# An attention and feed-forward kernel: the place of group 1's attention, of the splits of weights, and of second products behind first products

## The chip, the cores and the metric

The kernel runs on one core of one Trainium2 chip. The metric is the device time of one execution in microseconds (us). Before the change it is 775.43 us, the median of 3 runs (774.27 to 777.92).

## The reference

Attention with 4 sink keys and a causal window of 128 keys, then a feed-forward stage without gate. All arrays are float32 but the two weight matrices, which arrive as float64 (512 KB for a block of 128 x 512).

```python
# q, k, v: (4 batches, 8 heads, 768, 64)
scores = q @ k.T / 8;  keep = (key < n_sink) | (0 <= query - key < window)
a = softmax(where(keep, scores, -1e9));  attn = a @ v
x = attn, heads side by side             # (3072, 512)
h = x @ w_in                             # (3072, 2048)
g = h * erf(softplus(h))
out = g @ w_out                          # (3072, 512)
```

## The kernel before

**Groups and slots.** The 3072 tokens are 12 groups of 256 (three per batch). A group has 4 attention steps, one for each pair of heads (step s belongs to group s // 4), and 16 slots of the feed-forward stage, one for each block of 128 hidden columns. Slot m of the loop has the first product of block f = m % 16 of group m // 16 (`hidden`); every second slot the activation of two blocks (`act`); and the second product of slot m - 4 (`project`, LAG = 4). Ten slots of attention alone (LEAD) stand ahead, so the planner's slot number is a = m + 10.

**Two forms of the products.** Group 0's first products, and the second products of groups 0 and 1, are float32 matmuls (L606, L649). All others are made of three rounded (fp32r) matmuls each, of high and low parts (L610; L652 to L654). They need each weight block split in two: a cast to the high part on ScalarE and a subtraction on VectorE (`wsplit`, L527 and L528). Before that, the 32 blocks are converted from float64 bits to float32 by three VectorE instructions each (`wconv`, L511, L516, L519). Blocks 0 to 15 are w_in's, 16 to 31 w_out's. Splits 0 to 15 have the slots m = 11 to 26, splits 16 to 31 the slots m = 24 to 46 (`split`).

**A step of attention.** `prep` transposes q and k on TensorE (L281), ScalarE copies them to kq. `score` multiplies on TensorE (L329); VectorE merges halves (L341) and adds the mask with a row maximum (L346); ScalarE takes the exponent (L350). `norm` divides (L357 to L369; steps 4 to 7 have the four products on ScalarE, L363). `ptrans` transposes the probabilities (L381, L382); ScalarE copies them (L385, L390), GpSimd cuts triangles out of them (L395). `av` multiplies with v (L422). `xfin` makes x: for group 0 one copy (L435), for others a high part on ScalarE (L440) and a low part on VectorE (L441). Group g's first products read x of all its four steps, in 4 chunks of contraction, one chunk per step.

**What sets the order.** `pos(s)` is a step's slot, and `plan` holds the parts of a step with their slots. Steps 0 to 3 (NE = 4) have slots 0 to 3, with `av` three slots after `score` and `xfin` four. From step 4 on, the slots are 4 apart (5, 9, 13, 17, 21, ...), and `av` of step s stands directly before the scores of step s + 2 (AL = 2; `core`, L289). Each part gets a priority key by `at`: 256 times its slot, plus an offset by kind (O: scores -300, preparation -100, activation -400, first product 0, splits +300, second product +900). The build's planner lays out each engine's queue from these keys and from what it takes to be ready; each engine then works through its queue in that order. `follow(prev, ins)` ties an instruction behind another of the same queue, without a semaphore.

**Buffers.** First products have two PSUM tiles (tag h), each for two slots; a tile comes free when VectorE's first multiplication of the activation (L631, i = 0) has read it. Second products have two tiles (tag o), one group's; transposes, preparation and `av` share two (tag t). Weights, their splits and the inputs of groups 0 and 1 (k_early, q_early, v_early) share 33 buffers (wpool). SyncE issues all loads in one queue, among them copies of v to vz, which `av` reads: `next_dup` (L248, L250) for group 1, in slot 8.

Of the kernel before, what the change touches and what calls it, by code (L numbers as in the profile page):

```python
# [9 lines left out]
F32 = mybir.dt.float32  # L10
# [3 lines left out]
AF = mybir.ActivationFunctionType  # L14
ALU = mybir.AluOpType
# [14 lines left out]
CC = (-0.3597576685435788, 7.2931830957863735, 0.5777779046187317)  # L30
CK = 0.018644221205607978
CS = CK ** (1 / 6)
# [7 lines left out]
NE, AL = 4, 2  # L40
# [12 lines left out]
def kernel(  # L53
# [11 lines left out]
    nc = tc.nc  # L65
# [3 lines left out]
    NPAIR = H // 2  # L69
# [8 lines left out]
    scale = 1.0 / math.sqrt(D)  # L78
# [8 lines left out]
    b_a = [CS * a for a in CA]  # L87
# [38 lines left out]
    wf, wt = {}, {}  # L126
# [4 lines left out]
    def fast_path():  # L131
        with ExitStack() as st:
# [19 lines left out]
                out=kw[:, :256], in0=rf[:, :256], scalar=0.0, in1=kw[:, :256], op0=ALU.is_ge, op1=ALU.mult  # L152
# [27 lines left out]
            xp, early = {}, {}  # L180
# [108 lines left out]
            def core(s):  # L289

                prev = None
                late = s - AL >= NE
                if late:
                    prev = av(s - AL)
                if s < NSTEP:
                    score(s, prev)
# [150 lines left out]

            def pos(s):

                return s if s < NE else 4 * s - 11  # L450

            plan = {}
            for s in range(NSTEP + AL):
                if s < NSTEP:
                    for what, fn, a in (
                        ("prep", prep, pos(s) - (3 if s < NE or s >= 2 * NPAIR else 1)), ("norm", norm, pos(s) + 1), ("ptrans", ptrans, pos(s) + 2),
                        ("load", load, pos(s) - 4),
                    ):
                        if what == "load":
                            if s < 2 * NPAIR:  # L460
                                continue
                            plan.setdefault(a, []).append(("load", load_v, s))
                        plan.setdefault(max(a, 0 if what == "prep" else -1), []).append((what, fn, s))
                    if s >= 2 * NPAIR:
                        plan.setdefault(pos(s) - 2, []).append(("dup", dup, s))
                    if s // NPAIR % GPB < GPB - 1:
                        plan.setdefault(pos(s) + (2 if s < NE else 1), []).append(("kcopy", kcopy, s))
                plan.setdefault(pos(s), []).append(("core", core, s))
                if s < NE:
                    plan.setdefault(pos(s) + 3, []).append(("av", av, s))  # L470
                    plan.setdefault(pos(s) + 4, []).append(("xfin", xfin, s))
                elif s - AL >= NE:
                    plan.setdefault(pos(s) + 1, []).append(("xfin", xfin, s - AL))
            STAGES = ("av", "xfin", "norm", "ptrans", "kcopy", "prep", "core", "dup", "load")

# [44 lines left out]
                    out=ti, in0=w[:, :, 0], scalar=29, in1=ti, op0=ALU.logical_shift_right, op1=ALU.bitwise_or  # L520
                )

            def wsplit(n):

                t = wf[n]
                d = wt[n] = wpool.tile([P, 2, DM], F32R, tag="wo", name=f"wt_{n}")
                nc.scalar.copy(d[:, 0, :], t)  # L527
                nc.vector.tensor_tensor(d[:, 1, :], t, d[:, 0, :].bitcast(F32), op=ALU.subtract)  # L528

            def wblock(n):  # L530
                if n < 16:
# [4 lines left out]
            mlp = make_mlp(work, ps_h, ps_o)  # L536
            wn, wl = 0, W0
            gs = {}
# [13 lines left out]
            for m in range(-LEAD, NG * NF + LAG + 2):  # L552
                a = m + LEAD
                live = 0 <= m < NG * NF
                if live:
                    g, f = divmod(m, NF)
                    if f % 2 == 0:
                        hp = mlp.hid_tile(m)
                    if f > 0:
                        with at(a, "hid"):  # L560
                            mlp.hidden(hp, xp[g], f)
                attn(a)
                w = m - LAG
                if 0 <= w < NG * NF:
                    g2, f2 = divmod(w, NF)
                    with at(a, "proj"):
                        mlp.project(gs[w // 2], g2, f2)
                    if f2 == NF - 1:
                        for i in range(2):
                            r0 = (g2 * 2 + i) * P  # L570
                            with at(a, "res"):
                                nc.sync.dma_start(out[r0 : r0 + P, :], mlp.result(g2, i))
                if live:
                    if f == 0:
                        with at(a, "hid"):
                            mlp.hidden(hp, xp[g], f)
                    if f % 2 == 1:
                        with at(a, "act"):
                            gs[m // 2] = mlp.act(hp, m, g < 2)

                while wn < 32 and a >= 1 and (wn < (0, 1, 3, 5)[a - 1] if a < 5 else wn < 2 * a - 4 or need(order[wn]) <= m + W1):
                    with at(a, "wc"):
                        wconv(order[wn], wn)
                    wn += 1
                    with at(a, "wl"):
                        for n in order[wl : wn + WQ]:
                            wload(n)
                            wl += 1
                for n in split.get(m, ()):
                    with at(a, "ws"):  # L590
                        wsplit(n)

    class make_mlp:
        def __init__(self, work, ps_h, ps_o):
            self.work, self.ps_h, self.ps_o = work, ps_h, ps_o
            self.acc = {}

        def hid_tile(self, m):
            return self.ps_h.tile([P, 2, GT], F32, tag="h", name=f"h_{m}")
# [1 line left out]
        def hidden(self, hp, xt, f):  # L601
            j, fs = f // 4, slice(f % 4 * P, f % 4 * P + P)
            o = hp[:, f % 2, :]
            if len(xt) == 1:
                for c in range(NC):
                    nc.tensor.matmul(o, wf[NC * j + c][:, fs], xt[0][:, c, :], start=(c == 0), stop=(c == NC - 1))  # L606
                return
            ops = [(c, *e) for c in range(NC) for e in ((0, 0), (0, 1), (1, 0))]
            for m, (c, p, e) in enumerate(ops):
                nc.tensor.matmul(  # L610
                    o, wt[NC * j + c][:, p, fs], xt[e][:, c, :], start=(m == 0), stop=(m == len(ops) - 1)
                )

        def act(self, hp, m, whole=False):
            work = self.work
            h = hp.rearrange("p a t -> p (a t)")
            r = work.tile([P, 512], F32, tag="r", bufs=1, name=f"r_{m}")
            if whole:
                acc = work.tile([P, 2, 512], F32, tag="g", bufs=2, name=f"gf_{m}")[:, 0, :]
            else:  # L620
                acc = None
            nc.scalar.activation(r, h, AF.Tanh, bias=b_t, scale=0.5)  # L622
            nc.scalar.activation(r, r, AF.Square, bias=b_v, scale=-0.5)  # L623
            nc.scalar.activation(r, r, AF.Square, bias=b_r)  # L624
            for i in range(3):
                u = work.tile([P, 512], F32, tag="u", bufs=UB, name=f"u{i}_{m}")
                nc.scalar.activation(u, r, AF.Square, bias=b_a[i], scale=CS)  # L627
                x = h if i == 0 else acc
                if acc is None:
                    acc = u  # L630
                nc.vector.scalar_tensor_tensor(out=acc, in0=u, scalar=CC[i] * CS**2, in1=x, op0=ALU.add, op1=ALU.mult)  # L631
            if whole:
                return (acc,)
            gt = work.tile([P, 2, 512], F32R, tag="g", bufs=2, name=f"g_{m}")
            gh, gl = gt[:, 0, :], gt[:, 1, :]
            nc.vector.tensor_copy(gh, acc)  # L636
            nc.gpsimd.tensor_tensor(gl, acc, gh.bitcast(F32), op=ALU.subtract)  # L637
            return gh, gl

        def project(self, gt, g, f):  # L640
            if f == 0:
                for i in range(2):
                    self.acc[g, i] = self.ps_o.tile([P, DM], F32, tag="o", name=f"o_{g}_{i}")
            for i in range(2):
                o = self.acc[g, i]
                n0 = (f % 2) * GT + i * P
                ws = slice(n0, n0 + P)
                if len(gt) == 1:
                    nc.tensor.matmul(o, gt[0][:, ws], wf[16 + f], start=(f == 0), stop=(f == NF - 1))  # L649
                    continue  # L650
                gh, gl = gt
                nc.tensor.matmul(o, gh[:, ws], wt[16 + f][:, 0, :], start=(f == 0), stop=False)  # L652
                nc.tensor.matmul(o, gh[:, ws], wt[16 + f][:, 1, :], start=False, stop=False)  # L653
                nc.tensor.matmul(o, gl[:, ws], wt[16 + f][:, 0, :], start=False, stop=(f == NF - 1))  # L654

# [151 lines left out]
```

## Time and profile before

| | |
|---|---|
| median of 3 runs | 775.43 us |
| the profiled execution, whole | 773.4 us |
| its span, first to last instruction | 771.6 us |
| TensorE busy | 728.0 us (94%) |
| VectorE busy | 496.0 us (64%) |
| ScalarE busy | 549.2 us (71%) |
| GpSimd busy | 202.4 us (26%) |
| mean granted TensorE clock | 0.978 |

Busy times are of one profiled execution. TensorE's matmuls are pipelined, so that the length of one says less than the distance from one start to the next. "Idle before" is an engine's empty time ahead of an instruction, with what ended it. A share over the whole span mixes the opening, in which weights come in and are converted, with ten groups that look alike.

### The profile page before, as it was taken

How to read it: one execution, taken by the hardware profiler on the slowest of the kernel's cores; microseconds unless marked ns; L12 is line 12 of the kernel's file. 1: busy time of each engine (PE TensorE's matmuls, PEld its weight loads, DVE VectorE, ACT ScalarE, POOL GpSimd, SP SyncE). 2: the span in 40 equal slices, each digit the busy share in tenths (PEclk: the TensorE clock that was granted, in tenths of full speed). 3: DMA queues.
4: the chain of work that ended last, by engine and by line, in shares of the span. 5: the costliest groups of instructions: out<-in, count | busy, mean ns of one | idle time of the engine just before them, and what ended most of it. 6: DMA issues, size and time to landing. Idle time of an engine off the chain costs nothing. (4 is left out here: it accounts for less than half of the span.)

```text
span 771.6 us, 16346 instructions
## 1 busy us (share of the span) xinstructions
PE 728.0 (94%) x5808; PEld 603.5 (78%) x5808; DVE 496.0 (64%) x1375; ACT 549.2 (71%) x1293; POOL 202.4 (26%) x281
## 2 busy tenths in 40 slices
PE   6689946999999999999999999999999999999997
PEld 3456624776788888888888888888888888888895
DVE  7999983566477476476476476476476476576352
ACT  4476855887597588588598587587597597597572
POOL 1220102201233332232242242242242242242221
PEclk9899969999999999999999999999999999999999
DMA  9999002211122122122222222212212212210000
GB/s 196 257 330 364 15 0 45 66 39 34 41 69 52 49 57 56 48 51 51 55 51 61 53 51 59 51 47 55 55 48 61 55 49 57 52 34 1 29 1 32
DMA packets 115112, 53.59 MB, mean 69 GB/s; under 512 B 93840, under 2 KB 107664, under 8 KB 115024
## 3 DMA queue, kind: packets, MB, share of 16 engines
q1 hardware_dynamic: 114192, 52.33, 25.8%
q8 instruction: 49, 0.80, 0.4%
q14 instruction: 39, 0.32, 0.1%
q10 hardware_dynamic: 832, 0.13, 0.1%
HBM read 38.54 MB, written 6.29 MB: 58 GB/s over the span
## 5 line engine op out<-in xcount | busy, mean ns | idle before, releaser
L610 PE MATMUL h<-xh,wt 128*128 128x256 f32 x1408 | 273.0, 284 | 10.3 <-DVE gf L631 7.3
L610 PEld LDWEIGHTS h<-xh,wt 128*128 128x128 f32 x1408 | 223.3, 188 | 19.0 <-DVE gf L631 7.2
L610 PE MATMUL h<-xl,wt 128*128 128x256 f32 x704 | 198.3, 283 | 0.0
L627 ACT ACTIVATE u<-r 128x512 f32<-128x512 f32 x288 | 161.5, 622 | 9.9 <-DVE gf L631 2.2
L637 POOL TENSOR_TENSOR g<-u,g 128x512 fp32r<-128x512 f32 x80 | 104.1, 1302 | 241.7 <-DVE g L636 216.7
L610 PEld LDWEIGHTS h<-xl,wt 128*128 128x128 f32 x704 | 132.3, 188 | 4.8 <-issue 1.0
L395 POOL TENSOR_SCALAR_AFFINE_SELECT pz<-pa 64x256 f32<-64x256 f32 x96 | 52.1, 543 | 313.2 <-ACT pa L385 310.0
L652 PE MATMUL o<-wt,g 128*128 128x512 f32 x320 | 129.5, 405 | 0.1
L631 DVE SCALAR_TENSOR_TENSOR u<-u,u 128x512 f32<-128x512 f32 x160 | 119.0, 744 | 15.9 <-ACT u L627 1.0
L653 PE MATMUL o<-wt,g 128*128 128x512 f32 x320 | 127.9, 400 | 0.0
L654 PE MATMUL o<-wt,g 128*128 128x512 f32 x320 | 124.5, 399 | 0.3 <-POOL g L637 0.2
L631 DVE SCALAR_TENSOR_TENSOR u<-u,h 128x512 f32<-128x512 f32 x80 | 54.9, 686 | 81.0 <-ACT u L627 75.5
L350 ACT ACTIVATE pst<-pst,neg 128x144 f32<-128x144 f32 x192 | 77.6, 406 | 15.1 <-DVE neg L346 13.2
L622 ACT ACTIVATE r<-h 128x512 f32<-128x512 f32 x96 | 57.0, 594 | 41.5 <-PE h L610 34.1
L654 PEld LDWEIGHTS o<-wt,g 128*128 128x128 f32 x320 | 59.0, 188 | 12.7 <-POOL g L637 0.6
L653 PEld LDWEIGHTS o<-wt,g 128*128 128x128 f32 x320 | 60.2, 188 | 11.0
L652 PEld LDWEIGHTS o<-wt,g 128*128 128x128 f32 x320 | 60.2, 188 | 10.7 <-issue 0.3
L649 PE MATMUL o<-wf,gf 128*128 128x512 f32 x128 | 60.2, 613 | 3.2 <-DVE gf L631 3.2
L624 ACT ACTIVATE r<-r 128x512 f32<-128x512 f32 x96 | 60.7, 633 | 2.7
L623 ACT ACTIVATE r<-r 128x512 f32<-128x512 f32 x96 | 61.0, 635 | 2.0
L636 DVE CAST g<-u 128x512 fp32r<-128x512 f32 x80 | 36.4, 455 | 36.1 <-PE o L654 32.8
L441 DVE TENSOR_TENSOR xl<-av,xh 128x256 fp32r<-128x256 f32 x44 | 18.5, 420 | 55.5 <-ACT xh L440 54.9
(85 smaller groups left out, 968.3 us busy)
## 6 DMA issues: line engine op xcount, KB each, us to landing
ws<-in_moe_w_in_dram SPq DMA_DIRECT2D x16, 512.0 KB, 6.7
ws<-in_moe_w_out_dram SPq DMA_DIRECT2D x16, 512.0 KB, 9.0
out_dram<-ot SPq DMA_DIRECT2D x24, 256.0 KB, 2.2
v<-in_v_dram SPq DMA_DIRECT2D x56, 96.0 KB, 2.4
q<-in_q_dram SPq DMA_DIRECT2D x80, 64.0 KB, 2.1
k<-in_k_dram SPq DMA_DIRECT2D x80, 64.0 KB, 2.1
vz<-v SPq DMA_DIRECT2D x80, 64.0 KB, 2.1
kq<-kq SPq DMA_DIRECT2D x28, 64.0 KB, 1.9
```

Of the source, the lines that this page charges most:

```text
L350: nc.scalar.activation(y, y, AF.Exp, bias=d["neg"][:, i, h : h + 1], scale=-1.0, accum_out=d["sum"][:, i, h : h + 1])
L610: nc.tensor.matmul(o, wt[NC * j + c][:, p, fs], xt[e][:, c, :], start=(m == 0), stop=(m == len(ops) - 1))
L622: nc.scalar.activation(r, h, AF.Tanh, bias=b_t, scale=0.5)
L623: nc.scalar.activation(r, r, AF.Square, bias=b_v, scale=-0.5)
L624: nc.scalar.activation(r, r, AF.Square, bias=b_r)
L627: nc.scalar.activation(u, r, AF.Square, bias=b_a[i], scale=CS)
L631: nc.vector.scalar_tensor_tensor(out=acc, in0=u, scalar=CC[i] * CS**2, in1=x, op0=ALU.add, op1=ALU.mult)
L637: nc.gpsimd.tensor_tensor(gl, acc, gh.bitcast(F32), op=ALU.subtract)
L649: nc.tensor.matmul(o, gt[0][:, ws], wf[16 + f], start=(f == 0), stop=(f == NF - 1))
L652: nc.tensor.matmul(o, gh[:, ws], wt[16 + f][:, 0, :], start=(f == 0), stop=False)
L653: nc.tensor.matmul(o, gh[:, ws], wt[16 + f][:, 1, :], start=False, stop=False)
L654: nc.tensor.matmul(o, gl[:, ws], wt[16 + f][:, 0, :], start=False, stop=(f == NF - 1))
```

## The change

There are three parts. First, group 1's four steps (4 to 7) get the slots 6, 9, 12, 15 instead of 5, 9, 13, 17; their preparation moves to the slots 4, 4, 5, 6 (before: 4, 8, 12, 16); their `av` stands three slots after their scores, and `xfin` four (slots 10, 13, 16, 19), as for group 0, where before `av` waited for the scores of two steps later (`xfin` in the slots 14, 18, 22, 26). Second, the two instructions of a split of slot m are tied behind the last square (ScalarE) and the last multiplication (VectorE) of an activation some two to three slots earlier. Third, for slots m of group 2 and later, except the first of each group, the first matmul of each half of the second product of slot m - 4 is tied behind the last matmul of slot m's first product.

```diff
-                late = s - AL >= NE
+                late = s - AL >= 2 * NPAIR
...
-                return s if s < NE else 4 * s - 11
+                return s if s < NE else 3 * s - 6 if s < 2 * NPAIR else 4 * s - 11
...
-                        ("prep", prep, pos(s) - (3 if s < NE or s >= 2 * NPAIR else 1)), ("norm", norm, pos(s) + 1), ("ptrans", ptrans, pos(s) + 2),
+                        ("prep", prep, max(4, s - 1) if NE <= s < 2 * NPAIR else pos(s) - 3), ("norm", norm, pos(s) + 1), ("ptrans", ptrans, pos(s) + 2),
...
-                if s < NE:
+                if s < 2 * NPAIR:
                     plan.setdefault(pos(s) + 3, []).append(("av", av, s))
                     plan.setdefault(pos(s) + 4, []).append(("xfin", xfin, s))
-                elif s - AL >= NE:
+                elif s - AL >= 2 * NPAIR:
...
-            def wsplit(n):
+            def wsplit(n, m):
...
-                nc.scalar.copy(d[:, 0, :], t)
-                nc.vector.tensor_tensor(d[:, 1, :], t, d[:, 0, :].bitcast(F32), op=ALU.subtract)
+                x, y = mlp.mark[(m - 1) // 2 - 1]
+                follow(x, nc.scalar.copy(d[:, 0, :], t))
+                follow(y, nc.vector.tensor_tensor(d[:, 1, :], t, d[:, 0, :].bitcast(F32), op=ALU.subtract))
...
-                            mlp.hidden(hp, xp[g], f)
+                            ahead = mlp.hidden(hp, xp[g], f)
...
-                        mlp.project(gs[w // 2], g2, f2)
+                        mlp.project(gs[w // 2], g2, f2, lambda ins: follow(ahead if live and f and g >= 2 else None, ins))
...
+            if isinstance(m, int):
+                self.mark[m // 2] = sq, pr
...
-        def project(self, gt, g, f):
+        def project(self, gt, g, f, behind=lambda ins: ins):
...
-                nc.tensor.matmul(o, gh[:, ws], wt[16 + f][:, 0, :], start=(f == 0), stop=False)
+                behind(nc.tensor.matmul(o, gh[:, ws], wt[16 + f][:, 0, :], start=(f == 0), stop=False))
```

## Rows read from the trace of the kernel before

**Rows 1.** The page's busy tenths of TensorE and VectorE and the granted clock, in 40 slices of 19.3 us.

```profile
PE   6689946999999999999999999999999999999997
...
DVE  7999983566477476476476476476476476576352
...
PEclk9899969999999999999999999999999999999999
```

**Rows 2.** Busy time by stage: stretch, its length, busy us (instructions) of TensorE, its weight loads, VectorE, ScalarE and GpSimd, granted clock, share of the DMA engines, GB/s.

```profile
0.00:41.40 41.40, 27.00 (x228) 17.20 (x228) 35.15 (x131) 18.58 (x62) 10.33 (x25) 0.92 0.94 238
41.40:97.70 56.30, 53.47 (x242) 35.85 (x243) 55.88 (x121) 42.91 (x93) 8.03 (x8) 0.97 0.66 223
97.70:146.90 49.20, 31.79 (x260) 22.00 (x260) 29.01 (x89) 27.74 (x77) 6.98 (x15) 0.79 0.10 24
146.90:204.40 57.50, 57.50 (x413) 39.99 (x408) 34.63 (x101) 43.79 (x106) 7.55 (x14) 1.00 0.20 48
204.40:765.97 561.57, 558.21 (x4672) 488.50 (x4670) 341.38 (x937) 415.58 (x956) 169.46 (x220) 1.00 0.20 48
```

**Rows 3.** TensorE's instructions in order of time, 97 to 141 us: start, us, engine, line, operation, tiles, shape, count, and idle time before with what ended it.

```profile
97.70 0.35 PE L610 MATMUL h<-xh,wt 128*128 128x256 f32 x1 [0.92 <-DVE gf L631]
...
104.68 0.58 PE L610 MATMUL h<-xh,wt 128*128 128x256 f32 x1 [6.38 <-DVE gf L631]
...
108.88 9.41 PE L649 MATMUL o<-wf,gf 128*128 128x512 f32 x16 [3.20 <-DVE gf L631]
...
121.17 0.99 PE L329 MATMUL ps<-kq 64*64 64x208 f32 x16
...
126.59 0.33 PE L381 MATMUL tp<-ident,pst 128*128 128x128 f32 x1 [3.15 <-ACT pst L363]
...
140.83 0.48 PE L610 MATMUL h<-xh,wt 128*128 128x256 f32 x2
```

**Rows 4.** VectorE's groups of instructions in the stretch 97.7 to 147.9 us: count, busy us, mean ns, idle before.

```profile
L528 DVE TENSOR_TENSOR wt<-wf,wt 128x512 fp32r<-128x512 f32 x18 | 12.2, 717 | 9.4 <-ACT wt L527 9.3
L346 DVE CUSTOM_DVE_ANT_0 pst<-ps,mask 128x144 f32<-128x144 f32 x16 | 4.0, 304 | 0.1
L341 DVE COPY_PREDICATED ps<-tri,ps 64x256 f32<-64x256 int8 x8 | 3.4, 431 | 0.8 <-PE ps L329 0.6
...
L441 DVE TENSOR_TENSOR xl<-av,xh 128x256 fp32r<-128x256 f32 x3 | 1.2, 416 | 4.2 <-ACT xh L440 4.2
```

**Rows 5.** ScalarE in order of time, 88 to 105 us.

```profile
88.01 5.84 ACT L527 CAST wt<-wf 128x512 fp32r<-128x512 f32 x11
...
104.06 0.63 ACT L627 ACTIVATE u<-r 128x512 f32<-128x512 f32 x1
```

**Rows 6.** The casts of splits (L527) on ScalarE alone, by stage: stretch, length, busy us (count), clock, DMA.

```profile
41.40:97.70 56.30, 7.59 (x14) 0.97 0.66 223
97.70:111.00 13.30, 4.20 (x7) 0.58 0.00 0
...
146.90:204.40 57.50, 4.32 (x7) 1.00 0.20 48
```

**Rows 7.** Distances between starts on TensorE at full clock: 14 matmuls of a float32 second product (66.58 to 72.59); `av`, scores and preparation of one step (431.02 to 433.30); 24 matmuls of first products (435.94 to 438.77); the transposes of probabilities (439.71, 440.14).

```profile
66.58 6.17 PE L649 MATMUL o<-wf,gf 128*128 128x512 f32 x14
72.59 3.62 PE L606 MATMUL h<-xf,wf 128*128 128x256 f32 x16
...
431.02 0.55 PE L422 MATMUL av<-pa,v 128*64 128x128 f32 x8
...
433.30 0.48 PE L652 MATMUL o<-wt,g 128*128 128x512 f32 x1
...
435.94 0.40 PE L610 MATMUL h<-xh,wt 128*128 128x256 f32 x2
...
438.77 0.39 PE L654 MATMUL o<-wt,g 128*128 128x512 f32 x1
...
439.71 0.60 PE L381 MATMUL tp<-ident,pst 128*128 128x128 f32 x4
440.14 0.27 PE L382 MATMUL ts<-ident,snk 128*128 128x128 f32 x1
```

**Rows 8.** A boundary between two groups in the steady part, all engines in order of time.

```profile
429.53 0.39 PE L652 MATMUL o<-wt,g 128*128 128x512 f32 x1
...
432.49 0.42 DVE L441 TENSOR_TENSOR xl<-av,xh 128x256 fp32r<-128x256 f32 x1 [4.89 <-ACT xh L440]
...
440.81 0.39 PE L610 MATMUL h<-xh,wt 128*128 128x256 f32 x1 [0.40 <-DVE u L631]
```

**Rows 9.** The table of TensorE's waits over the whole span: the row of the first products behind a PSUM tile in use (waiting instruction, releaser: us in total, times, longest).

```profile
PE h L610 <- DVE u L631: 3.0, 8, 0.4
```

**Rows 10.** The instructions on vz: the issues of `next_dup` (count, ns of an issue, first and last start), and the time from issue to landing of all copies to vz (shortest, median, longest).

```profile
L250 SPq DMA_DIRECT2D vz<-v_early x2: 461/698/935, 51.6 to 53.8; - x2
...
DMA to landing us min/median/max: 1.5/2.1/10.6
```

**Rows 11.** GpSimd and VectorE in order of time, 81 to 85 us.

```profile
81.69 1.76 POOL L395 TENSOR_SCALAR_AFFINE_SELECT pz<-pa 64x256 f32<-64x256 f32 x2 [21.92 <-ACT pa L385]
...
83.19 1.61 DVE L516 SCALAR_TENSOR_TENSOR wf<-ws,wf 128x512 int32<-128x512 int32 x2
```

**Rows 12.** All 32 conversions of one kind (ns: shortest, median, longest; first and last start).

```profile
L516 DVE SCALAR_TENSOR_TENSOR wf<-ws,wf x32: 668/692/893, 20.9 to 94.5; 128x512 int32<-128x512 int32 x32
```

More of the change, by code (lines that the diff above doesn't have):

```diff
@@ L590, in fast_path @@
                     with at(a, "ws"):
-                        wsplit(n)
+                        wsplit(n, m)
     class make_mlp:
@@ L595, in __init__ @@
             self.work, self.ps_h, self.ps_o = work, ps_h, ps_o
-            self.acc = {}
+            self.acc, self.mark = {}, {}
         def hid_tile(self, m):
@@ L609, in hidden @@
             for m, (c, p, e) in enumerate(ops):
-                nc.tensor.matmul(
+                last = nc.tensor.matmul(
                     o, wt[NC * j + c][:, p, fs], xt[e][:, c, :], start=(m == 0), stop=(m == len(ops) - 1)
                 )
+            return last
         def act(self, hp, m, whole=False):
@@ L626, in act @@
                 u = work.tile([P, 512], F32, tag="u", bufs=UB, name=f"u{i}_{m}")
-                nc.scalar.activation(u, r, AF.Square, bias=b_a[i], scale=CS)
+                sq = nc.scalar.activation(u, r, AF.Square, bias=b_a[i], scale=CS)
                 x = h if i == 0 else acc
@@ L630, in act @@
                     acc = u
-                nc.vector.scalar_tensor_tensor(out=acc, in0=u, scalar=CC[i] * CS**2, in1=x, op0=ALU.add, op1=ALU.mult)
+                pr = nc.vector.scalar_tensor_tensor(out=acc, in0=u, scalar=CC[i] * CS**2, in1=x, op0=ALU.add, op1=ALU.mult)
+            if isinstance(m, int):
+                self.mark[m // 2] = sq, pr
             if whole:
```

## The prediction

> **What bounds the kernel now.** I read four views in this order. The page's busy tenths [rows 1] show TensorE at nine tenths or more from the eighth slice to the last but one. Ahead of that, behind an opening of "66899", stands one hole, the digits "46" of the sixth and seventh slices, about 96 to 135 us; the granted clock falls there too. So the steady part is bounded by TensorE itself, and what can be won lies before some 147 us. The sums by stage [rows 2] put numbers to this. From 146.90 to 765.97 us TensorE is idle for 3.4 of 619 us. In the stretch 97.70 to 146.90 it is busy for 31.79 of 49.2 us, at a granted clock of 0.79: part of the stretch is at the lower level (1.2 GHz), so that even the busy time is stretched. Just before, from 41.40 to 97.70, VectorE is full (55.88 of 56.3) and TensorE nearly so (53.47).
>
> TensorE in order of time [rows 3] shows what the hole is made of. Group 1's first products begin at 97.70 and stop after a few matmuls; the bulk starts at 140.83. Between lie the scores of step 7 (121.17) and transposes that wait for ScalarE: x of group 1 isn't ready, since its last two attention steps run one after the other with nothing beside them. They are late because VectorE and ScalarE were given something else first. ScalarE casts 11 splits in a row from 88.01 on, and the last square of an activation of group 0 is done only after 104.06 [rows 5]; 21 of the 32 casts are done by 111 us [rows 6], when group 1 needs four of them to begin. VectorE subtracts 18 splits after 97.70, 12.2 us of its time [rows 4]. The idle times of 0.92, 6.38 and 3.20 us at 97.70, 104.68 and 108.88 all end with group 0's activations, which stood in that queue.
>
> **What the hole is worth.** I price its work at full clock by the distances of [rows 7]. 16 float32 second products at (72.59 - 66.58)/14 = 0.43 us make 6.9. 48 matmuls of first products (slots 16 to 19) at (438.77 - 435.94)/24 = 0.118 make 5.7. Four attention steps, each with `av`, scores and preparation of 433.30 - 431.02 = 2.28 and transposes of 0.43 + 0.27 = 0.70, make 11.9. That is 24.5 us of work in 49.2 us [rows 2]: 24.7 us are lost, 17.4 as idle time and the rest to the clock. This is the most that the first two parts of the change can give back there.
>
> **Part 1, group 1's attention.** No instruction is added. Step 5 to 7's preparation no longer stands behind the transposes of the step before, and `av` no longer behind the scores of two steps later; x of group 1 is due in slot 19 instead of 26. The work goes under the stretch from 41.40 on. Its costs, where none can gain unless an end below 0 says so:
> - Three preparations go ahead of group 0's first products. TensorE is idle for 14.4 us of the first 41.40 and ScalarE for 22.8 [rows 2], which hides them. Ends -1.5 (they fill idle time) and +2 (the copies of group 0's x queue behind them on ScalarE). I take 0.
> - VectorE's share of steps 6 and 7 moves ahead of 97.70: per step (4.0 + 3.4)/4 + 1.2/3 = 2.25 us for the three larger kinds [rows 4], 4.5 for both, some 6 with the small kinds. The engine is full there, so conversions and activations behind them come later; TensorE is covered as far as these were ahead of use. Subtractions that leave the stretch give back 0.68 each. Ends -1 and 6.4; I take 3.
> - `av` of step 4 reads vz, whose copies for group 1 are issued at 51.6 to 53.8 us and land up to 10.6 us later [rows 10], at 64.4. The SyncE queue and slot 8 of these copies are unchanged, and the slot of this `av` falls from 13 to 9. TensorE works its queue in order: score, products and transposes behind a waiting `av` wait as well. Ends 0 and 6; I take 1.5. Freed earlier, k_early and q_early give buffers back to the loads of weights, which can only help.
> - GpSimd's cuts of steps 6 and 7 now run beside a full VectorE. At 83.19, under a GpSimd run, two conversions take 1.61 us [rows 11] against 0.692 each in the median and 0.893 at the longest [rows 12]: 0.2 us more for each instruction that is caught. Some five per step make 2 us for two steps. Ends 0 and 2; I take 1.
>
> The Trainium skill's GPSIMD Engine Reference, section Specifications, says that GpSimd shares its SBUF interfaces with VectorE, with contention for VectorE instructions that have two SBUF inputs. By that rule the subtractions and activations beside the cuts would slow down too; the trace agrees as far as the 0.893 against 0.692 goes, and the sum would end 2 us later than without any contention.
>
> **Part 2, the splits.** The ties keep splits 0 to 7 behind activations of group 0 and send the others, of which some 13 were done by 111 us, into group 1's time. This frees ScalarE around 88 to 107 us and lets the last two activations of group 0 go as their products end, so the 16 second products follow at once. Splits 8 to 23 then fall into group 1: 16 casts against 7 in 146.90 to 204.40 [rows 6], 9 x 0.62 = 5.6 us more on ScalarE, 49.4 of 57.5 us [rows 2]. That is 86%, close enough for some waits: ends 0 and 6, I take 1.5. At the start of group 1 both PSUM tiles are filled after four slots and the next waits for the first activation; the 6.9 us of group 0's second products cover that if they are still there. Ends 0 and 3, I take 1.
>
> **Part 3, second products behind first products.** In most slots the keys (offset 900, so 3.5 slots) put a second product behind the first product of four slots ahead anyway, and the tie changes nothing. It bites at a group's end: second products of blocks 13 to 15 now stand before the next group's first products of slots 1 to 3 (one of them at 429.53, before x is whole at 432.49 + 0.42) [rows 8], and will stand behind them. Then the new group's first activation starts earlier, and the wait of 0.40 us at 440.81 for a PSUM tile [rows 8] goes; there are 8 of these, 3.0 us in all [rows 9]. For filling the time before x is whole, three of four chunks of the first products of four slots remain. Ends: a gain of 4 (ten boundaries at 0.40) and a loss of 42 (18 matmuls at (439.71 - 438.77)/4 = 0.235 [rows 7], 4.2 us a boundary, all uncovered, at ten boundaries). I take a gain of 2, near the measured wait, because 432.91 lies before the 433.30 at which TensorE is through with scores and preparation.
>
> **The sum.** 24.7 - (0 + 3 + 1.5 + 1 + 1.5 + 1) + 2 = 24.7 - 8.0 + 2 = 18.7 us. The profiled execution took 773.4 us, so 754.7; the median shown is 775.43, 2.0 above it, so I predict 756.7, rounded to 757. What is late next is VectorE until about 106 us, then TensorE.
>
> **Rivals.**
> - *The hole shrinks only.* VectorE has no slack under 41.40 to 97.70 and the costs of parts 1 and 2 come at their upper ends, two thirds of them: 16 us in place of 8, part 3 nothing. 773.4 - 24.7 + 16 = 764.7, with the 2.0 about 767 (762 to 771). For it: 55.88 of 56.3 busy. Against it: 12.2 us of subtractions leave the queue behind.
> - *The change doesn't do what it says.* The scores of steps 4 to 7 move by only +1, 0, -1 and -2 slots, and the planner's queues may hold them as late as before: 775. For it: step 7, of slot 17, was scored at 121.17, long after the first product of slot 26 (m = 16) had begun at 97.70 [rows 3], so slots alone don't place it. Against it: that was the serial order of transposes, preparation and `av`, which is gone.
> - *Slower: part 3 drains TensorE at every boundary.* Its place is between the last matmul that needs no fourth chunk and the moment x is whole, in each of the ten boundaries; its price up to 4.2 us each. It decides from 18.7/10 = 1.9 us a boundary. At half the price, 21 us, the time is 773.4 - 24.7 + 8.0 + 21 + 2.0 = 780; at the full price 801. For it: one second product is used just there now, at 429.53. Against it: the four slots' three chunks hold 36 matmuls, 4.2 us, of which part is used already.
>
> **How the numbers follow.** My forecast has a chance of 0.58 (748 to 762), the smaller gain 0.24, no effect 0.08, slower 0.10. Less than 0.5% (3.9 us) can't be told from no change: faster 0.82, same 0.08, slower 0.10. The low end takes all 24.7 us, part 3's 4 and no cost: 773.4 - 28.7 + 2.0 = 746.7, hardly to be had, so 748; the high end takes in the smaller gain: 771.
>
> **What would show it.** Right: scores of step 7 before 97 us, a granted clock near 1.00 from 97 to 147 us, no run of 11 casts, fewer than ten casts by 100 us, and the wait at a PSUM tile after each boundary gone. Wrong: first products of group 1 still starting after 115 us; TensorE idle around 58 to 64 us behind vz for more than 3 us; a new wait of first products for xl at each boundary; ScalarE above nine tenths in group 1 with TensorE waiting for it.

## The result, and the profile after

The changed kernel takes 750.03 us (median of 4 runs, 748.57 to 750.50) against 776.67 us before (4 runs, 774.27 to 778.52): a ratio of 0.9655, with a 95% interval of 0.9622 to 0.9689. The profiled execution took 750.17 us, 23.2 less than the 773.4 of before. The predicted 757 was 7 us too high; the range of 748 to 771 holds the time. One execution of part 1 alone, at 893.04 us and a mean granted clock of 0.752, is left out of that kernel's median and ratio below.

The busy tenths of the changed kernel, which answer to [rows 1]:

```profile
PE   6589899999999999999999999999999999999996
...
DVE  7999896565786665666665665666576576475252
...
PEclk9899999999999999999999999999999999999999
```

The hole at the sixth and seventh slices is gone, and so is the drop of the clock. VectorE's line is no longer full up to the sixth slice and then empty: it has been evened out. Busy time by stage, which answers to [rows 2]; the columns are the same:

```profile
0.00:41.40 41.40, 26.48 (x212) 17.19 (x212) 35.38 (x132) 19.22 (x63) 10.84 (x25) 0.92 0.94 243
41.40:97.70 56.30, 50.85 (x316) 34.56 (x317) 53.47 (x134) 39.73 (x102) 21.19 (x17) 0.97 0.70 225
97.70:146.90 49.20, 49.20 (x334) 34.45 (x333) 35.88 (x95) 40.84 (x95) 4.01 (x8) 1.00 0.17 41
146.90:204.40 57.50, 55.83 (x431) 40.61 (x430) 36.56 (x106) 44.02 (x110) 10.75 (x18) 1.00 0.22 52
```

From 97.70 to 146.90 TensorE is busy for all of 49.20 us at a clock of 1.00 (31.79 and 0.79 before). Ahead of it, its idle time has grown from 2.8 to 5.5 us, and GpSimd's busy time has grown from 8.03 to 21.19 us for 17 instructions. TensorE in order of time, which answers to [rows 3]:

```profile
61.29 0.99 PE L329 MATMUL ps<-kq 64*64 64x208 f32 x16
...
84.60 0.34 PE L422 MATMUL av<-pa,v_early 128*64 128x64 f32 x4 [1.92 <-POOL pa L395]
...
107.82 0.68 PE L611 MATMUL h<-xh,wt 128*128 128x256 f32 x1
...
194.86 0.40 PE L656 MATMUL o<-wt,g 128*128 128x512 f32 x1
```

Step 7 is scored at 61.29 us instead of 121.17, group 1's first products start at 107.82 and TensorE runs through from there (before, a few started at 97.70 and the bulk at 140.83), and group 2's second products start at 194.86. Before, those stood here:

```profile
213.97 0.47 PE L652 MATMUL o<-wt,g 128*128 128x512 f32 x1
```

At both points the same work is done, so they can be compared: the count of score matmuls (L329) by then is 240 in both. First the trace before, then after; the columns are stretch, length, TensorE busy (count) and weight loads busy (count) of this line alone, clock, DMA.

```profile
0.00:213.97 213.97, 18.30 (x240) 9.83 (x240) 0.93 0.44 125
213.97:765.97 552.00, 32.58 (x528) 18.27 (x528) 1.00 0.20 47
```

```profile
0.00:194.86 194.86, 17.20 (x240) 9.37 (x240) 0.97 0.49 137
194.86:742.90 548.04, 32.59 (x528) 18.29 (x528) 1.00 0.20 48
```

The opening has become 213.97 - 194.86 = 19.1 us shorter, and the rest, from there to the last matmul, 552.0 - 548.0 = 4.0 us. TensorE's waits over the span of the changed kernel, of which the second row answers to [rows 9]:

```profile
PE av L422 <- POOL pa L395: 7.7, 7, 1.9
...
PE h L611 <- DVE u L633: 0.3, 1, 0.3
```

The wait for a PSUM tile after each boundary is gone (3.0 us before). What is new is that `av` waits for GpSimd's cuts, 7.7 us in all. The casts of splits by stage, which answer to [rows 6]:

```profile
41.40:97.70 56.30, 0.49 (x1) 0.97 0.70 225
97.70:111.00 13.30, 3.92 (x8) 1.00 0.09 21
111.00:146.90 35.90, 5.53 (x10) 1.00 0.19 48
146.90:204.40 57.50, 5.83 (x10) 1.00 0.22 52
```

One cast begins before 97.70 us where 14 did; the run of 11 is no more.

### The profile page after: what moved, and what is told of

Read it like the earlier page. It is cut to its first block, busy times and chain, and to the rows that moved or that the text cites. A ratio compares the mean times of both kernels' runs of the same rounds, so it can differ in the third digit from the quotient of the medians.

```text
span 748.5 us, 16369 instructions
## 1 busy us (share of the span) xinstructions
PE 720.6 (96%) x5808; PEld 598.4 (80%) x5808; DVE 493.9 (66%) x1375; ACT 548.6 (73%) x1293; POOL 212.1 (28%) x281
## 5 line engine op out<-in xcount | busy, mean ns | idle before, releaser
L611 PE MATMUL h<-xh,wt 128*128 128x256 f32 x1408 | 277.9, 286 | 0.3 <-DVE u L633 0.3
L641 POOL TENSOR_TENSOR g<-u,g 128x512 fp32r<-128x512 f32 x80 | 105.9, 1323 | 342.8 <-DVE g L640 336.1
L629 ACT ACTIVATE u<-r 128x512 f32<-128x512 f32 x288 | 161.5, 622 | 11.8 <-DMA out_dram<-ot 3.0
L633 DVE SCALAR_TENSOR_TENSOR u<-u,u 128x512 f32<-128x512 f32 x160 | 125.9, 787 | 14.3
L395 POOL TENSOR_SCALAR_AFFINE_SELECT pz<-pa 64x256 f32<-64x256 f32 x96 | 60.2, 627 | 179.3 <-ACT pa L385 176.0
L624 ACT ACTIVATE r<-h 128x512 f32<-128x512 f32 x96 | 56.6, 589 | 18.7 <-PE h L611 13.7
L385 ACT COPY pa<-tp 128x512 f32<-128x512 f32 x48 | 28.1, 586 | 36.1 <-PE tp L381 34.8
```

The lines of the kernel that those rows point to most:

```text
L395: nc.gpsimd.affine_select(out=out, in_=x, pattern=[[0, 2], [0, 2], [-sg, HP]], compare_op=op, fill=0.0, base=0, channel_multiplier=sg,)
L611: last = nc.tensor.matmul(o, wt[NC * j + c][:, p, fs], xt[e][:, c, :], start=(m == 0), stop=(m == len(ops) - 1))
L629: sq = nc.scalar.activation(u, r, AF.Square, bias=b_a[i], scale=CS)
L633: pr = nc.vector.scalar_tensor_tensor(out=acc, in0=u, scalar=CC[i] * CS**2, in1=x, op0=ALU.add, op1=ALU.mult)
```

## Experiments: one part alone, and two together

The first four kernels ask whether the parts add up.

**Part 3 alone.** The kernel before, with the ties of second products:

```diff
-                        mlp.project(gs[w // 2], g2, f2)
+                        mlp.project(gs[w // 2], g2, f2, lambda ins: follow(ahead if live and f and g >= 2 else None, ins))
...
```

> The kernel before with the ties of second products behind first products alone. Theory (the ties remove the 0.40 us wait for a PSUM tile at each group boundary, whatever the opening does): 3 to 4.5 us faster than before, ratio 0.994 to 0.996, the hole at 97 to 147 us unchanged. Rival (the gain after group 2 comes from the earlier attention, not from the ties): ratio 1.000, or slower if the boundary drains.

Measured: 773.39 us beside 776.15, ratio 0.9959 (0.9937 to 0.9980): 2.8 us, a little under the 3 that I had expected. In the table of waits of this kernel the PSUM tile's row has shrunk as in the changed kernel:

```profile
PE h L610 <- DVE u L632: 0.2, 1, 0.2
```

Group 2's second products start at 220.39 us in this trace:

```profile
220.39 0.47 PE L653 MATMUL o<-wt,g 128*128 128x512 f32 x1
```

From there to the last matmul it takes 548.2 us, as the changed kernel does (548.0; before 552.0). The ties act without the other parts, and no boundary drains. The rival that the steady part's gain came from the earlier attention falls. The opening of this execution is 6.4 us longer than that of the trace before, although the tie is only for group 2 and later; the last section comes back to this.

**Part 1 alone**, the placement of group 1's attention, splits free:

```diff
-                return s if s < NE else 4 * s - 11
+                return s if s < NE else 3 * s - 6 if s < 2 * NPAIR else 4 * s - 11
...
-                if s < NE:
+                if s < 2 * NPAIR:
...
```

> The kernel before with group 1's attention moved alone, splits untied. Theory (two causes that add up: serial attention, and splits ahead of group 0's last activations): 12 to 16 us faster, ratio 0.979 to 0.985; casts of splits still in one run near 88 us and activations of blocks 12 to 15 still late. Rival (one chain only, the splits only fill time that is empty anyway): 19 us faster, ratio 0.975.

Measured: 763.26 us (median of five), ratio 0.9837 (0.9805 to 0.9869). ScalarE in order of time:

```profile
93.00 2.16 ACT L527 CAST wt<-wf 128x512 fp32r<-128x512 f32 x4
95.60 3.73 ACT L527 CAST wt<-wf 128x512 fp32r<-128x512 f32 x7
99.99 1.14 ACT L527 CAST wt<-wf 128x512 fp32r<-128x512 f32 x2
102.61 3.20 ACT L527 CAST wt<-wf 128x512 fp32r<-128x512 f32 x6
```

19 casts in some 13 us still stand in the way of group 0's last activations, and TensorE's first products wait 6.0 us for these after 85 us. Attention alone gives 12.9 us, not 19.

**Part 2 alone**, the ties of splits:

```diff
-                nc.scalar.copy(d[:, 0, :], t)
+                x, y = mlp.mark[(m - 1) // 2 - 1]
+                follow(x, nc.scalar.copy(d[:, 0, :], t))
...
```

> The kernel before with the splits tied alone, attention as before. Theory (two causes): the row maxima of step 6 (at 110.66 us before) come near 98 us, and 6 to 10 us are won, ratio 0.987 to 0.992, with steps 7 to x still one after the other. Rival (attention alone is the cause): under 3 us, ratio over 0.996.

Measured: 769.34 us, ratio 0.9900 (0.9864 to 0.9935), 6.8 us. The row maxima of step 6 came at 105.77 us, not near 98: earlier than 110.66, but the step's place was missed.

**Parts 1 and 2 without 3**, the changed kernel without the ties of second products.

> The changed kernel without the ties of second products. Theory: 19 us faster than before (the distance at the start of group 2's second products, 214.0 against 194.9 us), ratio 0.975, and the 0.40 us waits for a PSUM tile back at the boundaries, 3 us in all. Rival (the ties of part 3 do nothing, the steady part gained from elsewhere): as the changed kernel, ratio 0.966.

Measured: 756.79 us, ratio 0.9745 (0.9715 to 0.9775): 19.4 us, and 12.9 + 6.8 = 19.7 is the sum of the two alone, each known to some 2.5 to 3 us by its interval. So the hole had two causes, serial attention and splits ahead of the last activations. That they add up exactly isn't shown. By the traces, at the start of group 2's second products, part 1 alone has won 13.9 us (200.08 against 213.97) and both 19.1; in the traces with a long opening (see the last section) part 2 alone has won 10.9 (209.47 against the 220.39 of part 3 alone) and both 21.1. So the part that comes second may be worth less than alone: 5.2 for the splits, 10.2 for the attention, each from single executions. The wait for a PSUM tile is back in this kernel:

```profile
PE h L611 <- DVE u L632: 3.5, 9, 0.4
```

Between the medians of this kernel and of the changed one lie 6.8 us, more than the 4.0 that the steady part shows and the 2.8 of part 3 alone. The traces part them. Group 2's second products start here at

```profile
199.25 0.40 PE L655 MATMUL o<-wt,g 128*128 128x512 f32 x1
```

and from there to the last matmul it takes 552.4 us. Without the ties this rest is 552.0 to 552.5 us in four traces (before, part 1 alone, part 2 alone, parts 1 and 2), with them 548.0 to 548.2 in six (part 3 alone, the changed kernel twice, and three of its variants below). So the ties are worth 3.8 to 4.5 us. The other 2 to 3 us lie in the opening, which differs by more than that from one execution to the next (last section).

## Experiments: which edits of part 1 and of part 2 carry it

**Preparation late again**, all else as changed:

```diff
-                        ("prep", prep, max(4, s - 1) if NE <= s < 2 * NPAIR else pos(s) - 3), ("norm", norm, pos(s) + 1), ("ptrans", ptrans, pos(s) + 2),
+                        ("prep", prep, pos(s) - 1 if NE <= s < 2 * NPAIR else pos(s) - 3), ("norm", norm, pos(s) + 1), ("ptrans", ptrans, pos(s) + 2),
```

> The changed kernel with the preparation of steps 4 to 7 one slot ahead of the scores again (slots 5, 8, 11, 14), all else as changed. Theory (preparation behind the transposes of the step before is a link of the serial chain): scores of steps 5 to 7 come 3 to 10 us later, 3 to 8 us slower, 753 to 758. Rival (the late av alone was the chain): 750, no difference.

Measured: 766.46 us, ratio 0.9869 (0.9834 to 0.9904), 16 us slower than the changed kernel, twice what I had expected. Scores of steps 5 to 7 on TensorE, in order of time, with the transposes of step 6 (L381) and the preparation of step 7 (L281) between the last two:

```profile
71.66 0.99 PE L329 MATMUL ps<-kq 64*64 64x208 f32 x16
...
105.61 0.99 PE L329 MATMUL ps<-kq 64*64 64x208 f32 x16
...
115.40 0.27 PE L381 MATMUL tp<-ident,pst 128*128 128x128 f32 x1
...
116.67 0.44 PE L281 MATMUL tqk<-ident,k_early 128*128 128x128 f32 x2 [0.56 <-ACT pz L390]
...
118.00 0.99 PE L329 MATMUL ps<-kq 64*64 64x208 f32 x16 [0.68 <-ACT kq L284]
```

They come as late as before, or later (60.81, 93.88 and 121.17 there), although the slots of scores and `av` are the new ones: the preparation of step 7 again stands behind the transposes of step 6. The time is about what parts 2 and 3 give without part 1 (769.34 less some 4, an estimate), so without the early preparation the rest of part 1 brought nothing.

**`av` late again**, preparation and scores as changed:

```diff
-                late = s - AL >= 2 * NPAIR
+                late = s - AL >= NE
...
```

> The changed kernel with av of steps 4 to 7 back before the scores of two steps later, preparation and scores as changed. Theory: xfin of step 7 falls to the scores of step 9, in slot 26, and the first products of group 1 wait for it: 5 to 10 us slower, 755 to 760. Rival (early preparation is all that matters): 750, no difference, or faster since av no longer waits for GpSimd.

Measured: 759.65 us, ratio 0.9792 (0.9753 to 0.9830), 9.6 us slower than the changed kernel. Here the last `av` of group 1 on TensorE:

```profile
122.33 1.12 PE L422 MATMUL av<-pa,v_early 128*64 128x64 f32 x12 [0.61 <-ACT pa L385]
...
126.70 0.56 PE L611 MATMUL h<-xh,wt 128*128 128x256 f32 x1
```

A few first products of group 1 start at 99.70, and most wait behind this `av` until 126.70. The scores of steps 6 and 7, which stand behind the `av` of steps 4 and 5 again, come at 69.41 and 94.79 (50.29 and 61.29 in the changed kernel). So both edits are needed.

**Only the splits of w_out tied:**

```diff
-                x, y = mlp.mark[(m - 1) // 2 - 1]
+                x, y = mlp.mark[(m - 1) // 2 - 1] if n >= 16 else (None, None)
```

> The changed kernel with only the splits of w_out (16 to 31) tied, those of w_in free. Theory (any run of splits ahead of group 0's last activations delays them): some ten casts of w_in stand in one run again, within the activation of blocks 12 and 13, which then ends 5 to 7 us later; 2 to 6 us slower than the changed kernel, 752 to 756. Rival (the w_out splits alone were in the way): 750, no difference.

Measured: 756.10 us, ratio 0.9751 (0.9712 to 0.9791), beside 750.21 of the changed kernel run again on the same chip. ScalarE, from the start of the activation of blocks 12 and 13 (L624) to its last squares (L629):

```profile
96.07 0.60 ACT L624 ACTIVATE r<-h 128x512 f32<-128x512 f32 x1 [2.59 <-PE h L607]
...
97.24 2.16 ACT L528 CAST wt<-wf 128x512 fp32r<-128x512 f32 x4
...
99.84 3.72 ACT L528 CAST wt<-wf 128x512 fp32r<-128x512 f32 x7
...
105.28 1.67 ACT L629 ACTIVATE u<-r 128x512 f32<-128x512 f32 x3
```

In the changed kernel the same activation starts at 96.05 and its squares at 100.56. So a run of w_in's splits delays them too, by 4.7 us here. How the 5.9 us between the medians come of it isn't shown: this trace, one with a long opening, has group 2's second products at 199.91, and the trace of the changed kernel with such an opening at 199.20.

## Experiments: what the cuts on GpSimd cost

**`av` and `xfin` of steps 4 to 7 one slot later:**

```diff
-                    plan.setdefault(pos(s) + 3, []).append(("av", av, s))
+                    plan.setdefault(pos(s) + (3 if s < NE else 4), []).append(("av", av, s))
...
```

> The changed kernel with the av and xfin of steps 4 to 7 one slot later (four and five slots behind the scores). Theory (GpSimd's cuts, starved by VectorE, end up to several us after TensorE reaches av; one slot more covers it): TensorE's waits for GpSimd fall from 7.7 us to under 4 us and the time by 2 to 4 us, to some 747. Rival (x of group 1 is on the path to its first products, so a later av only moves the idle time to their start): 750 or more, with a new wait of first products for xl or xh.

Measured: 748.59 us, ratio 0.9633 (0.9595 to 0.9670); the waits for GpSimd are 5.7 us, not under 4, and no new wait of first products for xl or xh stands in the table. It was run once more, with the changed kernel beside it:

> The changed kernel with av and xfin of steps 4 to 7 one slot later, once more: if its 748.59 was a gain, 1 to 2 us under the changed kernel beside it; if it was chance, within 0.5 us of it.

> The changed kernel once more, beside the others on one chip: 750, 748.5 to 750.5.

Measured: 748.55 us, ratio 0.9651 (0.9621 to 0.9680), and the changed kernel 750.21, ratio 0.9674 (0.9640 to 0.9708). Twice 1.4 to 1.7 us less, with intervals that overlap: a small gain is likely, not shown. The two traces, both without the long opening, have group 2's second products at 193.29 and 192.90, the changed kernel's at 194.86. The waits for GpSimd are 6.8 us the second time, so their 0.9 us of less waiting don't explain it alone.

**Cuts of steps 0 to 7 on VectorE**, as products with a mask:

```diff
...
+                    if s < 2 * NPAIR:
+                        for j, out in enumerate((pz[hf, :, :, hf], x)):
+                            mk = cut[hf, j].rearrange("p (a b t) -> p a b t", a=1, b=1).broadcast_to([HP, 2, 2, HP])
+                            nc.vector.tensor_tensor(out, x, mk, op=ALU.mult)
+                        continue
```

> The changed kernel with the cuts of steps 0 to 7 made by VectorE as products with a 0/1 mask (four per step, 64 x 256), not by GpSimd. Theory (the cost is GpSimd's starvation, single cuts of up to 6.4 us): the waits for GpSimd before 100 us go, VectorE gets 32 instructions of some 0.35 us, 11 us, of which some 5.5 us fall into the full stretch; the time falls by 1 to 5 us, to 745 to 749, and runs lie closer together. Rival (VectorE itself is the bound in the stretch): 5 us slower, some 755.

Measured: 755.75 us, ratio 0.9731 (0.9694 to 0.9767), 5.7 us slower: the rival was right. Its waits:

```profile
PE h L616 <- DVE gf L642: 6.6, 1, 6.6
...
PE ps L333 <- DVE neg L350: 3.4, 2, 2.4
PE h L616 <- DVE wf L520: 3.1, 1, 3.1
```

TensorE waits for VectorE instead. VectorE is busy for 53.47 of the 56.30 us from 41.40 to 97.70 in the changed kernel and for 55.46 here, so it had little room for cuts of 0.42 us each.

**VectorE waits for the last cut of a step:**

```diff
+                if NE <= s < 2 * NPAIR:
+                    hold = small.tile([P, 1], F32, tag="hold", bufs=2, name=f"hold_{s}")
+                    nc.vector.tensor_copy(hold[hi], pa[hi, 1, 1, P - 1 :])
```

> The changed kernel with one VectorE copy of 64 numbers per step 4 to 7 that reads the last cut's result, so that VectorE stops until GpSimd is done. Theory (a cut is long because VectorE runs without a gap): the longest cut falls from 6.4 us to under 2 us and TensorE's waits for GpSimd from 7.7 to under 5 us; VectorE loses 1 to 2 us a step in a stretch where it is full; the time is the same within 4 us, 747 to 754. Rival (the cuts are long of themselves, or because of DMA traffic): cuts of 3 us and more remain, VectorE waits through them, 5 to 10 us slower.

Measured: 746.11 us (744.88 to 749.72), ratio 0.9636 (0.9607 to 0.9665), the lowest median of all, with an interval that overlaps the changed kernel's. All cuts of one kind (ns: shortest, median, longest), and TensorE's waits, in this kernel:

```profile
L395 POOL TENSOR_SCALAR_AFFINE_SELECT pz<-pa x96: 411/417/2365, 17.1 to 674.6; 64x256 f32<-64x256 f32 x96
```

```profile
PE av L425 <- POOL pa L395: 3.7, 4, 2.3
```

In the changed kernel that row of cuts reads 411/417/6352. The waits fell as expected and the cuts nearly so (2.37 us, not under 2), but VectorE waited in only one of the four places, for 0.5 us. So the stop itself is not what shortened the cuts; VectorE's queue was laid out anew as well, and which of the differences did it isn't shown.

## Why the prediction was right, and where its sizes were off

**The bound and the mechanism** held. The loss was priced at 24.7 us; 19.1 came back in the opening. The parts were told apart as they are: VectorE full, TensorE waiting for group 1's x and for group 0's last activations, each with its own edit.

**The price of the hole** has one step's scores too many. It counts four steps with scores; 16 score matmuls (L329) make a step, and the trace before has three steps' scores there:

```profile
97.70:146.90 49.20, 3.97 (x48) 2.12 (x48) 0.79 0.10 24
```

Scores take 0.92 us at full clock (431.97 to 432.89), so the work is 23.6 us, and 25.6 us were lost, not 24.7.

**The costs of parts 1 and 2**, taken as 8.0, were 24.7 - 19.1 = 5.6 us by the price as it stands, 6.5 with 25.6 us lost. TensorE's idle time before 97.70 rose by 3.1 us (0.5 in the first 41.40, 2.6 after), and 1.7 us stand in 146.90 to 204.40: 4.8 us, and no row accounts for the rest. By terms:
- The preparations, at 0: right within the 0.5.
- VectorE's load, at 3: not to be seen as a wait of its own for much more than 1.4 us (0.92 and 0.47 us idle before scores at 50.29 and products at 51.75). The engine is even less full than before from 41.40 to 97.70 (53.47 against 55.88 us), with the splits gone from there.
- The copies to vz, at 1.5: nothing. The planner put the half of step 4's `av` that reads vz at 66.25 us, ten us behind the other half.
- GpSimd's cuts, at 1, came out differently in kind. I had priced how they slow VectorE. What happened is that a cut waits while VectorE runs without a gap, and `av` waits for the cut:

```profile
75.99 8.07 POOL L395 TENSOR_SCALAR_AFFINE_SELECT pz<-pa 64x256 f32<-64x256 f32 x2 [7.82 <-ACT pa L385]
```

`av` waits for cuts for 5.3 us after 40 us (1.68, 0.85, 0.41, 1.92 and 0.48); the first is group 0's and was 1.17 before, the others, 3.7 us, are new. Over the span these waits grew from 2.9 to 7.7 us, the largest new idle time.

- ScalarE in group 1, at 1.5: it is busy for 44.02 of 57.5 us, not 49.4, since group 1 begins earlier and its 10 casts there are spread out. The start of group 1, at 1: nothing, TensorE runs through from 107.82.

So that the sum of the costs came near is in part luck: terms that came to little or nothing made up for the cuts, which cost several times their price.

**Part 3**, taken as a gain of 2, gave 4.0 (3.8 to 4.5 over the traces), the end that I had bounded it with. I took half of it out of caution about a drain that no boundary shows.

**The offset between profile and median**, taken as 2.0 from one execution, was -0.1 for the changed kernel (750.03 against 750.17). Of the 6.7 us by which the sum was too high, 2.4 are the costs, 2.0 part 3, and 2.1 this offset. That last one was no property of the kernel: one profiled execution of a kernel whose runs lie 4 us apart says little of its median, and the 773.4 of the one before lies under every other run of that kernel (773.51 at the lowest).

**The rivals.** The smaller gain (767) did not come: VectorE was less full than before, not more. The change did move what it says it moves, yet its rival had a point: slots alone would not have done it. With the new slots and the late preparation, step 7 is scored at 118.00. The drain at boundaries is excluded by part 3 alone, and by the steady part of the changed kernel, which became shorter.

## What to carry to other kernels

Where an engine is full, look at what stands in its queue ahead of the work that others wait for, and then at what follows later with the engine empty: here 12 us of split subtractions, most of them due later, stood ahead of what was due first. A serial chain can hide behind slot numbers; find the step at which one round waits for the round before (here preparation behind transposes, worth 16 us with the other edits in place) rather than moving the slots. Two causes of one hole can be told apart by undoing one at a time. Whether their gains add up takes traces of like executions: here the medians agree to 0.3 us, but that is closer than either gain is known.

## What the runs showed of the hardware that was not expected

GpSimd's cuts of 64 x 256 take 0.417 us in the median in the changed kernel, but 6.35 us at the longest, where VectorE runs without a gap (9.59 in the kernel with `av` late). VectorE's instructions keep their length until the cut gets in. The same program, profiled twice, shows it best. In the first, GpSimd and then VectorE in order of time:

```profile
32.19 2.30 POOL L395 TENSOR_SCALAR_AFFINE_SELECT pz<-pa 64x256 f32<-64x256 f32 x2 [7.63 <-ACT pa L385]
```

```profile
32.97 0.69 DVE L519 SCALAR_TENSOR_TENSOR wf<-ws,wf 128x512 int32<-128x512 int32 x1
33.76 0.46 DVE L511 TENSOR_SCALAR wf<-ws 128x512 int32<-128x512 int32 x1
34.14 1.70 DVE L516 SCALAR_TENSOR_TENSOR wf<-ws,wf 128x512 int32<-128x512 int32 x2
```

VectorE pauses for 0.1 us at 33.66, and the cuts get in; two conversions beside them take 1.70 us. In the second execution no such pause occurs:

```profile
32.27 5.92 POOL L395 TENSOR_SCALAR_AFFINE_SELECT pz<-pa 64x256 f32<-64x256 f32 x2 [7.63 <-ACT pa L385]
```

```profile
33.07 0.68 DVE L519 SCALAR_TENSOR_TENSOR wf<-ws,wf 128x512 int32<-128x512 int32 x1
33.67 0.41 DVE L511 TENSOR_SCALAR wf<-ws 128x512 int32<-128x512 int32 x1
34.00 1.28 DVE L516 SCALAR_TENSOR_TENSOR wf<-ws,wf 128x512 int32<-128x512 int32 x2
```

The two cuts end at 38.19 us, 0.8 us after VectorE's row of conversions does (36.75 + 0.68 = 37.43), and TensorE waits for them and the two that follow:

```profile
39.20 0.91 PE L422 MATMUL av<-pa,v_early 128*64 128x128 f32 x8 [4.71 <-POOL pa L395]
```

From here on the second execution stays behind. Its scores of step 4 start at 40.90 us (37.13 in the first), and group 2's second products at 199.20 (194.86):

```profile
199.20 0.40 PE L656 MATMUL o<-wt,g 128*128 128x512 f32 x1
```

The first execution took 750.17 us, the second 754.52. This is the long opening that was spoken of above. A cut pair of over 5 us at 32 us (5.9 to 6.0) stands in five of the profiled executions of this study: part 3 alone, part 2 alone, parts 1 and 2, the w_out ties, and the changed kernel the second time. In none of them does VectorE pause there. In the other eight with these cuts on GpSimd the pair takes 1.3 to 2.5 us, and in seven of them VectorE pauses beside it, for 0.06 to 0.8 us; the eighth, where VectorE waits for the last cut, shows no pause but one conversion of 0.64 us in place of 0.42. In four of the seven (before, part 1 alone, preparation late, and the first run of `av` one slot later) the profile says what ended the pause: the landing of a weight block. So a gap of a tenth of a microsecond on VectorE goes with some 4 us of the whole time. No run sets the gap on purpose, so that it is the cause is argued from these 13 traces, not shown by an edit. It is a likely reason why runs of one kernel here spread as they do (745.84 to 754.52 for the changed one), and why differences of 2 us between its variants can't be settled with six runs.
